# A decode attention and MLP kernel: output weights in longer runs, a reordered last stage, a weights-stationary second MLP layer

## The chip, the cores and the metric

One core of a Trainium2 chip. The time is the device time of one execution in microseconds (us). The kernel before is timed beside every experiment on the same chip, because chips and repeats differ by up to 2.5 us in 690.

"Span" is the stretch from the first to the last instruction in the trace. It is about 2 us shorter than the time.

## The reference, cut to what matters

One token for each of 8 sequences passes through an adaptive layer norm, an attention over a cache of 8192 keys, a projection, a second layer norm and a two-layer MLP.

```python
B, Sq, D = (8, 1, 512); Hq, Hkv, Sk, Dh = (32, 8, 8192, 128); F = 1792
sa, ca, ga, sb, cb, gb = split(_silu(c) @ w_mod)
h = _layernorm(x) * (1 + ca) + sa
q = (h @ wq)                                    # 32 heads, 4 share one key/value head
p = _softmax(q @ k_cache.T * Dh ** -0.5)        # k_cache, v_cache: 8 x 8 x 8192 x 128 bf16 each
x = x + ga * ((p @ v_cache) @ wo)               # wo: 4096 x 512
h = _layernorm(x) * (1 + cb) + sb
x = x + gb * (relu(h @ w1 + b1) ** 2 @ w2 + b2) # w1: 512 x 1792, w2: 1792 x 512
```

The two caches are 268 MB; everything else is about 15 MB.

## The kernel before

The caches are read in 64 units of 4 MB (two heads each; for every sequence four K units, then four V units) through a ring of four slots in SBUF. All large loads are issued by SyncE in one order. wo is loaded once, near the start, in rows of 1 KB:

```python
d_wo = dma("sync", s_wo, lambda e: e.dma_start(wo_sb[:], A_wo.rearrange("(h dh) n -> dh h n", dh=DH)))
```

An ordinary V unit takes 32 matmuls of 512 columns, an eviction to SBUF and four selecting matmuls. The very last V unit is loaded in four pieces (64, 32, 16 and 16 tiles) and done otherwise: 70 matmuls on an identity that do no work ("fillers", put there to keep TensorE's clock up), 128 value matmuls of 8 columns, and between them the part of the output projection that does not need the last unit:

```python
oT_ps = Obank[:, 0:8]
pe_fill(70)
t0 = 0
for i, t1 in enumerate(CH):                      # CH = (64, 96, 112, 128)
    for m in range(t0, t1):
        t = op("tensor", ... matmul(oT_ps, vt[:, m, :], lhs[:, p, 8 * m:8 * m + 8], ...), [loaded[n][i], ...])
    t0 = t1
    if i == 0:
        before_last()                            # 96 projection matmuls, bias matmuls
    elif i == 1:
        pe_fill(8)
# ... normalise, 32 late projection matmuls, layer norm, fillers, first MLP layer: cut ...
for f in range(FT):                              # second layer: the 8 tokens (padded to 64) stationary
    for cc in range(2):
        t = op("tensor", ... matmul(y_ps[64 * cc:64 * (cc + 1), :], hidT[:, f, :],
               W2v[:, f // 2, f % 2, 256 * cc:256 * (cc + 1)], ...), ...)
t = op("vector", ... tensor_tensor(y2, y_ps, gbN[:], ALU.mult), ...)      # gate
t = op("vector", ... tensor_tensor(out_sb, y2, x1N[:], ALU.add), ...)     # residual
# out: one half by SyncE's queue, one by ScalarE's
```

## Time and profile before

| | |
|---|---|
| time, median of 3 (range) | 690.26 us (690.22 to 691.19) |
| span of the profiled run | 689.1 us |
| HBM read | 283.66 MB, 412 GB/s over the span |
| last V unit but one, all of it landed | 656.2 us |
| from there to the end | 32.9 us |
| wo, 4 MB: from the landing of the unit ahead of it to its own | 42.0 to 54.4 us |
| W1, W2 landed / needed | 670.5, 675.0 / 681.4, 683.0 us |

The runs of this kernel fall into two groups, near 690 and near 691 us; the profiled run (690.87) is of the slower group, so its span is about 1 us above the typical one.

Two lines of the page, the span in 40 equal slices of 17.2 us: the busy tenths of the DMA engines and what they moved. Every slice but the first and the last two is full; the third, in which wo is loaded, moves less although it is as busy.

```profile
DMA  8999999999999999999999999999999999999970
GB/s 349 442 365 434 429 431 432 427 432 428 425 434 432 432 426 427 429 426 434 435 430 427 430 425 431 433 428 434 425 435 424 428 432 431 433 430 424 421 312 28
```

The timeline of the end, TensorE's main groups and the store. Columns: start, length of the group in us, engine, line of the program, operation, output and inputs, shape, count, and in brackets the idle time of that engine just before and what ended it.

```profile
656.27 3.60 PE L442 MATMUL PS<-ring,Pm 128*32 128x512 bf16 x32 [3.08 <-DMA ring<-in_A_v_cache_dram]
...
661.46 5.37 PE L340 MATMUL PS<-IDENT 128*128 128x128 bf16 x70
...
666.67 1.75 PE L506 MATMUL PS<-Pm,ring 128*128 128x8 bf16 x64
...
668.28 2.33 PE L478 MATMUL PS<-oTn,wo_sb 128*128 128x8 bf16 x87
672.62 0.38 PE L478 MATMUL PS<-oTn,wo_sb 128*128 128x8 bf16 x9 [2.01 <-issue]
...
676.75 1.02 PE L478 MATMUL PS<-oTn,wo_sb 128*128 128x8 bf16 x32 [0.29 <-DVE oTn L514]
...
681.41 1.68 PE L558 MATMUL PS<-hbT,ring 128*128 128x8 bf16 x56
...
683.02 3.20 PE L566 MATMUL PS<-ring,hidT 128*64 128x256 bf16 x28
...
687.18 0.33 SPq L573 DMA_DIRECT2D out_dram<-P_sb  x1
```

After the last wait for a V unit (first line) TensorE is never kept waiting long by another engine or a transfer: the rest is a serial tail (work in which each step waits for the one before). The fillers run from 661.46 to 666.8, although the first piece of the last V unit has landed at 661.1. Then comes a gap of 2.01 us marked "issue", in which TensorE waits for nothing that the profile shows, in the middle of a row of equal matmuls.

The trace also has a completion mark from each DMA engine for every transfer (read from the trace itself; no view prints them). They are not equal: half of the engines are done 11 us ahead of the other half, and the lag grows over the whole run, from 2 us at 83 us. It grows steadily: over the 58 units in between, the first mark comes every 9.71 us and the last every 9.87. (Marks of the last V unit but one, in us, sorted.)

```
644.6 644.7 644.7 644.7 645.2 645.3 646.2 648.9 | 654.1 655.6 655.6 655.7 655.7 655.8 656.0 656.2
```

Two more lines, of the timeline of SyncE's queue (the issue of w_mod) and of the list of transfers (wo: size, median time from issue to landing):

```profile
1.58 0.37 SPq L191 DMA_DIRECT2D ring<-in_w_mod_dram  x1
...
wo_sb<-in_A_wo_dram SPq DMA_DIRECT2D x1, 4096.0 KB, 50.8
```

### The profile page before, as it was taken

The numbers are of one execution on the slowest core, as the hardware profiler recorded it, in microseconds if no ns is written. First come the engines' busy times: TensorE is split into PE (matmuls) and PEld (weight loads), VectorE is DVE, ScalarE is ACT, GpSimd is POOL, SyncE is SP. The second block draws the span as 40 slices with busy tenths as digits, with TensorE's granted clock in tenths as the row PEclk, the third lists the DMA queues.
The fourth block names the chain that finished last, engine by engine and source line by source line (L and its number), as shares of the span: only waits on it lengthen the run. The fifth ranks groups of instructions, "written<-read, shape, count | busy, mean of one in ns | idle before, by whom it ended". The sixth has DMA issues, their size and how long they took to land.

```text
span 689.1 us, 16075 instructions
## 1 busy us (share of the span) xinstructions
PE 501.7 (73%) x7476; PEld 358.5 (52%) x7476; DVE 300.8 (44%) x557; ACT 235.1 (34%) x281; POOL 17.8 (3%) x67
## 2 busy tenths in 40 slices
PE   2393963897659965798639964698549975699577
PEld 2382731775237731676328741576317752477366
DVE  3161731567116741467216651367215671267302
ACT  1061620465006630366005640265204650156300
POOL 7200000000000000000000000000000000000000
PEclk9997976799659987899659996799857997699865
DMA  8999999999999999999999999999999999999970
GB/s 349 442 365 434 429 431 432 427 432 428 425 434 432 432 426 427 429 426 434 435 430 427 430 425 431 433 428 434 425 435 424 428 432 431 433 430 424 421 312 28
DMA packets 16022, 284.69 MB, mean 413 GB/s; under 512 B 1202, under 2 KB 5331, under 8 KB 6996
## 3 DMA queue, kind: packets, MB, share of 16 engines
q1 hardware_dynamic: 15940, 283.67, 96.7%
q8 instruction: 58, 0.95, 0.6%
q14 instruction: 8, 0.07, 0.0%
q10 hardware_dynamic: 16, 0.00, 0.0%
HBM read 283.66 MB, written 0.01 MB: 412 GB/s over the span
## 4 chain that ended last, share of the span: by engine, by line
PE 54%; DMA 39%; DVE 3%; ACT 2%; issue 1%; SPq 0%
PE PS L348 35%; DMA ring<-in_A_k_cache_dram 34%; PE PS L363 9%; DMA ring<-in_A_v_cache_dram 4%; PE PS L442 4%; PE PS L405 3%; PE PS L340 1%; ACT KTb L353 1%; ACT P_sb L396 1%; DVE Pm L418 1%; DVE m L368 1%; PE PS L423 1%; PE PS L478 1%; PE PS L506 0%; PE PS L566 0%
## 5 line engine op out<-in xcount | busy, mean ns | idle before, releaser
L353 ACT ACTIVATE KTb<-PS 128x1024 bf16<-128x1024 bf16 x192 | 196.5, 1024 | 384.2 <-PE PS L348 384.2
L348 PE MATMUL PS<-IDENT,ring 128*128 128x128 bf16 x4096 | 267.5, 227 | 49.2 <-DMA ring<-in_A_k_cache_dram 49.2
L348 PEld LDWEIGHTS PS<-IDENT,ring 128*128 128x128 bf16 x4096 | 246.9, 102 | 97.7 <-DMA ring<-in_A_k_cache_dram 52.3
L355 DVE COPY KTb<-PS 128x1024 bf16<-128x1024 bf16 x320 | 210.1, 688 | 149.5 <-PE PS L348 147.2
L442 PE MATMUL PS<-ring,Pm 128*32 128x512 bf16 x992 | 88.3, 519 | 51.7 <-DMA ring<-in_A_v_cache_dram 47.4
L363 PE MATMUL PS<-KTb,QTm 128*32 128x512 bf16 x1024 | 78.8, 384 | 4.5 <-ACT KTb L353 4.5
L451 DVE CAST O_sb<-PS 128x512 bf16<-128x512 f32 x31 | 21.4, 692 | 132.5 <-PE PS L442 132.5
L442 PEld LDWEIGHTS PS<-ring,Pm 128*32 128x32 bf16 x992 | 30.8, 121 | 90.2 <-DMA ring<-in_A_v_cache_dram 48.5
L454 PE MATMUL PS<-SEL,O_sb 128*128 128x8 bf16 x124 | 22.6, 182 | 30.4 <-DVE O_sb L451 24.8
L454 PEld LDWEIGHTS PS<-SEL,O_sb 128*128 128x128 bf16 x124 | 12.2, 98 | 59.5 <-DVE O_sb L451 46.1
L405 PE MATMUL PS<-IDENT,P_sb 128*64 128x128 bf16 x512 | 25.7, 276 | 10.3 <-ACT P_sb L396 10.0
L405 PEld LDWEIGHTS PS<-IDENT,P_sb 128*64 128x64 bf16 x512 | 22.1, 147 | 12.9 <-ACT P_sb L396 12.8
L396 ACT ACTIVATE P_sb<-PS,negm 128x512 bf16<-128x512 f32 x32 | 21.5, 685 | 18.9 <-DVE negm L393 18.9
L418 DVE COPY Pm<-PS 64x512 bf16<-64x512 bf16 x48 | 20.1, 421 | 16.6 <-PE PS L405 15.6
L363 PEld LDWEIGHTS PS<-KTb,QTm 128*32 128x32 bf16 x1024 | 15.4, 94 | 21.0 <-ACT KTb L353 8.5
L368 DVE TENSOR_REDUCE m<-PS 128x1 f32<-128x512 f32 x32 | 22.1, 689 | 6.6 <-PE PS L363 6.6
L457 DVE TENSOR_TENSOR oTn<-PS,rinv 128x8 bf16<-128x8 f32 x31 | 6.0, 194 | 31.1 <-PE PS L454 31.1
L542 ACT ACTIVATE std<-PS,epst 128x8 f32<-128x8 f32 x1 | 0.3, 267 | 33.8 <-PE PS L540 33.8
L415 ACT ACTIVATE Pm<-PS 64x512 bf16<-64x512 bf16 x16 | 9.4, 592 | 6.1 <-PE PS L405 5.8
L423 PE MATMUL PS<-rhs_r,ONES 128*128 128x32 f32 x16 | 4.2, 349 | 7.0 <-DVE rhs_r L421 7.0
L309 PE MATMUL PS<-haT,ring 128*128 128x8 bf16 x128 | 3.6, 168 | 7.4 <-DMA ring<-in_A_wq_dram 7.4
L391 PE MATMUL PS<-Dm,R 128*128 128x4 bf16 x8 | 1.4, 179 | 10.1 <-DVE Dm L389 10.1
(103 smaller groups left out, 115.1 us busy)
## 6 DMA issues: line engine op xcount, KB each, us to landing
ring<-in_A_k_cache_dram SPq DMA_DIRECT2D x32, 4096.0 KB, 34.3
ring<-in_A_v_cache_dram SPq DMA_DIRECT2D x31, 4096.0 KB, 29.2
ring<-in_A_wq_dram SPq DMA_DIRECT2D x1, 4096.0 KB, 20.6
wo_sb<-in_A_wo_dram SPq DMA_DIRECT2D x1, 4096.0 KB, 50.8
ring<-in_w_mod_dram SPq DMA_DIRECT2D x1, 3072.0 KB, 10.0
ring<-in_A_v_cache_dram SPq DMA_DIRECT2D x1, 2048.0 KB, 24.6
ring<-in_B_w_dram SPq DMA_DIRECT2D x1, 1792.0 KB, 22.5
ring<-in_A_v_cache_dram SPq DMA_DIRECT2D x1, 1024.0 KB, 26.7
```

What stands on the lines that cost most here:

```text
L348: t = op("tensor", lambda e, j=j, i=i: e.matmul(STG[j][:, i, :], src[:, 32 * k + 8 * j + i, :], IDENT[:, :], is_transpose=True), [loaded[n ...
L353: stg_free[j] = op("scalar", lambda e, j=j, dst=dst: e.activation(dst, STG[j], ACT.Copy), [t])
L355: stg_free[j] = op("vector", lambda e, j=j, dst=dst: e.tensor_copy(dst, STG[j]), [t])
L363: t = op("tensor", lambda e, hf=hf, q=q, rhs=rhs: e.matmul(PS[32 * q:32 * (q + 1), k, :], QTm[:, b, 2 * p + hf, :], rhs, start=(p == 0 and ...
L368: return op("vector", lambda e: e.tensor_reduce(m4[:, k:k + 1], bank(k), AX.X, ALU.max), [t])
L396: exps.append(op("scalar", lambda e, k=k: e.activation(P_sb[:, k, :], bank(k), ACT.Exp, bias=negm[:, 0:1], scale=inv_sqrt, accum_out=rs4[: ...
L405: t = op("tensor", lambda e, k=k, i=i, hf=hf, src=src: e.matmul(STG[k][64 * hf:64 * (hf + 1), i, :], src, IDENT[:, :], is_transpose=True, ...
L418: done.append(op("vector", lambda e, dst=dst, frm=frm: e.tensor_copy(dst, frm), [t, k_pm]))
L423: t = op("tensor", lambda e: e.matmul(tot_ps, ONES[:, :], rhs_r[:]), [t])
L442: t = op("tensor", lambda e, p=p, m=m, cg=cg, vt=vt, Obank=Obank: e.matmul(Obank[32 * cg:32 * (cg + 1), :], lhs[:, p, 32 * m:32 * m + 32], ...
L451: t = op("vector", lambda e, osb=osb, Obank=Obank: e.tensor_copy(osb, Obank), [t])
L454: t = op("tensor", lambda e, i=i, osb=osb, oT_ps=oT_ps: e.matmul(oT_ps, osb[:, i * 128:(i + 1) * 128], SEL[:, i, :], start=(i == 0), stop= ...
```

## The change

Its intent: waste less transfer time on wo, have less work between the last landing and the end, and make the second MLP layer cheaper. c and x are issued by ScalarE, so that SyncE starts with the large loads. Rows of wo are dealt out so that 24 of 32 heads come in runs of 4 KB; 16 small matmuls with a permutation (PERM) then bring the attention output into the same order. The early projection comes ahead of the last V unit, the fillers there go, and three quarters of that unit take the wide form of the other units. The second layer holds the weights stationary and streams 8 columns; its result is transposed at the end. The output went by two queues before as well; now each half has its own copy and leaves as soon as it is copied. The layer norm of the last stage keeps its fillers (20 instead of 16).

```diff
-        d_c = dma("sync", s_c, ...); d_x = dma("sync", s_x, ...)
+        d_c = dma("scalar", s_c, ...); d_x = dma("scalar", s_x, ...)
-        d_wo = dma("sync", s_wo, ... (wo_sb[:], A_wo.rearrange("(h dh) n -> dh h n", dh=DH)))
+        wo_e = wo_sb[:, 0:24, :].rearrange("p (g j) n -> p g (j n)", j=4)
+        d_woe = dma("sync", s_woe, ... (wo_e, A_wo[0:24 * DH, :].rearrange("(g p j) n -> p g (j n)", g=6, p=128)))
+        d_wo = dma("sync", s_wo, ... (wo_sb[:, 24:32, :], A_wo[24 * DH:, :].rearrange("(h dh) n -> dh h n", dh=DH)))
@@ last V unit (cut) @@
-                    pe_fill(70)
-                    # 128 matmuls of 8 columns; 96 early projections after the first 64; pe_fill(8)
+                    # 16 matmuls with PERM, copy to oP, 18 bias matmuls, 96 early projections from oP
+                    for m in range(24):          # 96 of 128 tiles, 512 columns each matmul
+                        t = op("tensor", ... matmul(bank(3)[32 * cg:32 * (cg + 1), :], lhs[...], vt[:, 4 * m:4 * m + 4, :], ...))
+                    t = op("vector", ... tensor_copy(osb, bank(3)), [t])
+                    direct(96, 112, 2, True, False)
+                    # 4 selecting matmuls on osb
+                    t = direct(112, 128, 3, False, True)
@@ second layer and output (cut) @@
-            for cc in range(2): matmul(y_ps[64 * cc:...], hidT[:, f, :], W2v[..., 256 * cc:256 * (cc + 1)], ...)
+            for k in range(KT): matmul(yT_ps[:, k, :], W2v[..., k * 128:(k + 1) * 128], hidT[:, f, :], ...)
+        # gate and residual on 128 x 32, four transposes, two copies (VectorE, ScalarE), two stores
```

## The prediction

> **What bounds it now.** The DMA page strip is at 9 tenths from the second slice to 659 us, 425 to 435 GB/s, 284 MB: the kernel streams the caches at the transfer limit. By the landing marks in the trace, half of the 16 DMA engines land 11 to 12 us after the other half at the end (last-but-one V unit: 644.6 against 656.2 us); the slow half sets the pace. After that landing there is a serial tail of 32.9 us (656.2 to 689.1, the timeline). Its parts: V matmuls 3.6, eviction and selection to 661.8; 70 filler matmuls 661.5 to 666.8, although the last V unit's first piece landed at 661.1; 160 small matmuls; a gap of 2.0 us marked "issue" at 670.6, which coincides with a 16 KB instruction fetch at 670.1 to 671.2; last values and late projection to 677.8; normalisation to 680.9; first MLP layer 681.4 to 683.1; second layer (28 matmuls of 256 columns) to 686.2; two vector operations to 687.15; store and end 1.9. W1 and W2 land at 670.5 and 675.0, needed at 681.4 and 683.0: not critical. The granted clock is 0.50 from 653 to 664 and after 673 (windows).
>
> **The change, step by step.**
> 1. Start: c and x leave SyncE's queue; the w_mod issue moves from 1.58 to about 0.8 us. DMA-bound, so 0.75 us earlier throughout. The Trainium skill (DMA: Bandwidth & Descriptors, "Issuing engines are not separate DMA queues") says that several issuers save only issue time; that is all I count.
> 2. wo: now 12.4 us for 4 MB in 1 KB packets (slow engines, 42.0 to 54.4) against 9.8 for a K unit. Packets of 4 KB take 161 ns against 152 per 4 KB in the 32 KB packets. 3 MB so: 8.1 + 3.1 = 11.2 us. Gain 1.2 to 1.6.
>    Both shift the last-but-one V landing to about 654.05.
> 3. Tail from that landing T (at the half clock, 31 ns a small matmul): V and eviction as before to T+5.6; 16 permutation matmuls 1.0, vector copy 0.4, 96 projections 3.0: T+10.4; 24 V matmuls of 512 columns 2.6: T+13.1; eviction, selection, last 16 value matmuls, normalise: T+15.1; late projection T+16.35; normalisation and fillers about 3.4, first layer 1.7: T+21.4; second layer 56 x 31 ns = 1.75 instead of 3.2: T+23.2; two 32-column vector operations, transposes, copies 1.5 instead of 0.9; store 1.9: T+26.6. Removed on the path: the 70 fillers (5.3 us), most of the instruction-fetch gap. No V piece or weight becomes the wait: they land 2 us earlier too, and W1 keeps about 5 us, W2 about 3.
>
> Span 680.65 instead of 689.1: 8.4 us less. Nearly all of it is on the path: 2.2 from transfers, 6.3 from the tail.
>
> **Predicted: 681.8 us, 679.0 to 685.0 (8 in 10).** Faster by over 2% (under 676.5): 0.03; within 2%: 0.96; slower: 0.01.
>
> **What would show it.** w_mod issue near 0.8 us; wo in two transfers of together about 11 us; last-but-one V landing near 654; no "issue" gap over 1 us in the tail; L569 (second layer) near 1.8 us; landing to end near 26.6 us.
>
> **What would make it wrong.** Instruction fetches stalling TensorE again (the Trainium skill, Runtime: NRT & Kernel Launch, "Instruction fetch mechanics", gives 16 KB blocks of 256 instructions; the trace's 58 packets of 16 KB agree): 1 to 2 us more. A clock at full speed in the tail: 1.5 to 2 us less. W2 landing late if the transfers do not shift. The time saved on wo being absorbed if the fast engines rather than the slow ones profit.

## The result and the profile after

The changed kernel takes 680.42 us (median of 4, 680.02 to 680.49) against 690.24 (689.53 to 691.19) beside it. The ratio is 0.9856, interval 0.9839 to 0.9873. Ratios here are the mean time of one kernel's fast runs over that of the other's of the same rounds, so not quite the ratio of the medians. That is 9.8 us less, 1.4%, within 2% as forecast.

| | before | predicted | after |
|---|---|---|---|
| last V unit but one landed | 656.2 | 654.05 | 653.7 |
| from there to the end of the span | 32.9 | 26.6 | 24.2 |
| wo: landing of the unit ahead to its own | 12.4 | 11.2 | 10.6 |
| span | 689.1 | 680.65 | 677.9 |

The spans differ by 11.2 us, more than the times, because the profiled run of before was one of its slower ones. The sizes in time below come from medians, not from these two spans.

The same two lines of the page after (slices of 16.9 us). The third slice moves 400 GB/s instead of 365, and the end is filled better: the slice before the last has 393 instead of 312.

```profile
DMA  8999999999999999999999999999999999999994
GB/s 365 439 400 434 430 431 433 430 431 425 424 433 429 428 431 433 432 430 431 432 433 425 418 432 430 429 427 431 431 433 432 430 424 426 431 429 431 427 393 160
```

The timeline of the end, after:

```profile
653.78 3.15 PE L438 MATMUL PS<-ring,Pm 128*32 128x512 bf16 x32 [0.88 <-DMA ring<-in_A_v_cache_dram]
...
658.91 0.32 PE L476 MATMUL PS<-oTn,PERM 128*32 128x48 bf16 x16 [0.28 <-DVE oTn L453]
...
659.73 2.64 PE L492 MATMUL PS<-oP,wo_sb 128*128 128x8 bf16 x96
...
662.30 2.75 PE L508 MATMUL PS<-ring,Pm 128*32 128x512 bf16 x24
...
666.84 1.02 PE L525 MATMUL PS<-oTn,wo_sb 128*128 128x8 bf16 x32 [0.29 <-DVE oTn L520]
...
671.27 1.68 PE L561 MATMUL PS<-hbT,ring 128*128 128x8 bf16 x56
...
672.81 0.99 PE L569 MATMUL PS<-hidT,ring 128*128 128x8 bf16 x32
...
674.00 0.81 PE L569 MATMUL PS<-hidT,ring 128*128 128x8 bf16 x24 [0.19 <-DMA ring<-in_B_w_dram]
...
676.08 0.32 SPq L588 DMA_DIRECT2D out_dram<-out_sb  x1
```

The late projection starts at 666.84 instead of 676.75, and no gap marked "issue" stands in TensorE's way any more. The second layer takes 2.0 us instead of 3.2, with a wait of 0.19 us for the last piece of W2, which lands at 674.0.

The queue at the start and wo:

```profile
0.81 0.39 SPq L192 DMA_DIRECT2D ring<-in_w_mod_dram  x1
...
wo_sb<-in_A_wo_dram SPq DMA_DIRECT2D x1, 3072.0 KB, 45.5
wo_sb<-in_A_wo_dram SPq DMA_DIRECT2D x1, 1024.0 KB, 48.0
```

### The profile page after: what moved, and what is told of

It is laid out like the page before. It is cut to its first block, busy times and chain, and to the rows that moved or that the text cites. A ratio compares the mean times of both kernels' runs of the same rounds, so it can differ in the third digit from the quotient of the medians.

```text
span 677.9 us, 15869 instructions
## 1 busy us (share of the span) xinstructions
PE 496.7 (73%) x7372; PEld 352.5 (52%) x7372; DVE 298.4 (44%) x558; ACT 234.9 (35%) x280; POOL 16.7 (2%) x66
## 4 chain that ended last, share of the span: by engine, by line
PE 49%; DMA 45%; DVE 3%; ACT 2%; issue 1%; SPq 0%
DMA ring<-in_A_k_cache_dram 37%; PE PS L344 33%; PE PS L359 8%; DMA ring<-in_A_v_cache_dram 4%; DMA ring<-in_B_w_dram 4%; PE PS L438 3%; PE PS L401 3%; ACT KTb L349 1%; ACT P_sb L392 1%; DVE m L364 1%; PE PS L419 1%; DVE Pm L414 0%; DVE rinv L420 0%; DVE rhs_r L417 0%; DVE Dm L385 0%
## 5 line engine op out<-in xcount | busy, mean ns | idle before, releaser
L349 ACT ACTIVATE KTb<-PS 128x1024 bf16<-128x1024 bf16 x192 | 196.5, 1024 | 378.3 <-PE PS L344 378.3
L359 PEld LDWEIGHTS PS<-KTb,QTm 128*32 128x32 bf16 x1024 | 15.5, 94 | 21.1 <-ACT KTb L349 8.5
```

The source lines that it names most:

```text
L349: stg_free[j] = op("scalar", lambda e, j=j, dst=dst: e.activation(dst, STG[j], ACT.Copy), [t])
L359: t = op("tensor", lambda e, hf=hf, q=q, rhs=rhs: e.matmul(PS[32 * q:32 * (q + 1), k, :], QTm[:, b, 2 * p + hf, :], rhs, start=(p == 0 and ...
```

## The experiments

Twelve runs on the chip. e3 and e7 start from the kernel before, all others from the changed kernel. They ask three things: what each part is worth (e1, e2, e3, e7), what the "issue" gap is (e3, e7, e8), and whether the late half of the DMA engines sets the pace, and can be relieved (e4 to e6, e9, e11).

### e1: wo in 1 KB runs again

```diff
-        d_woe = dma("sync", s_woe, ... (wo_e, A_wo[0:24 * DH, :].rearrange("(g p j) n -> p g (j n)", ...)))
+        for j in range(4):     # same places in SBUF, rows of 1 KB
+            d_woe = dma("sync", s_woe, ... (wo_j[:, :, j, :], wo_r[:, :, j, :]))
```

> The changed kernel with the first 24 heads of wo in 1 KB runs again (four transfers, one for each row of a 4 KB run, same place in SBUF). Theory (short packets cost transfer time, and the slow half of the DMA engines is never short of work): wo takes 12.4 us instead of 10.6, the landing of the last-but-one V unit moves from 653.7 to about 655.4, the time is about 1.7 us longer than the changed kernel, ratio to before about 0.988. Rival (the ring of four slots absorbs it): landing and time as in the changed kernel, ratio 0.9856.

Measured: 681.73 us (681.21 to 681.89), ratio 0.9872. The changed kernel's eight runs (not taken beside this one; four of them surely on another chip) are all between 680.02 and 680.53. wo took 11.9 us (41.4 to 53.3) instead of 10.6, and the last V unit but one landed at 655.1 instead of 653.7. So the landing moved by 1.4 us and the time by 1.3. Nothing was absorbed by the ring: transfer time saved 600 us before the end is still there at the end.

### e2: c and x on SyncE's queue again

```diff
-        d_c = dma("scalar", ...); d_x = dma("scalar", ...)
+        d_c = dma("sync", ...); d_x = dma("sync", ...)
```

> The changed kernel with c and x issued by SyncE again. Theory: w_mod is issued near 1.58 us instead of 0.81, all landings 0.7 us later, time 0.7 us longer, ratio about 0.9866. Rival: the start does not matter, because x then lands earlier (7.9 us in the changed kernel, 2.7 before) and gives the time back: within 0.2 us.

Measured: 680.75 us (680.60 to 680.95), ratio 0.9859. In its timeline the issue of w_mod is back where it was:

```profile
1.56 0.37 SPq L192 DMA_DIRECT2D ring<-in_w_mod_dram  x1
```

The last V unit but one landed at 654.4, 0.7 us later; the time is 0.3 us longer. The landing followed the theory and the time about half of it. The difference is too near the spread of repeats to say where the rest went. x did land late in the changed kernel (7.9 us instead of 2.7), but nothing waited for it that mattered.

### e3: the kernel before without its 70 fillers

```diff
-                    pe_fill(70)
```

> The kernel before without its 70 filler matmuls ahead of the last V unit. Theory (they lie on the path, and the 2.0 us gap is an instruction fetch tied to a place in the instruction stream): the first value matmul starts near 661.8 instead of 666.7; at the half clock the following 160 matmuls take about 0.9 us longer; the gap is not after 87 projection matmuls any more but 221 matmuls after the last selection, or gone; time 4 to 6 us shorter, ratio about 0.993. Rival (the fillers pay for themselves by the full clock they bring, the gap belongs to the projection): time within 1 us of before, the gap again after the 87th projection matmul.

Measured: 684.41 us (684.15 to 684.56) against 690.19, ratio 0.9912. That is 5.8 us, more than half of what the whole change brings, from deleting one line. Its timeline:

```profile
661.20 1.85 PE L505 MATMUL PS<-Pm,ring 128*128 128x8 bf16 x64
...
662.91 2.70 PE L478 MATMUL PS<-oTn,wo_sb 128*128 128x8 bf16 x96
...
668.03 0.32 PE L505 MATMUL PS<-Pm,ring 128*128 128x8 bf16 x5
...
669.11 0.86 PE L505 MATMUL PS<-Pm,ring 128*128 128x8 bf16 x27 [0.75 <-issue]
```

Two things are seen here. First, the value matmuls start at 661.2 instead of 666.67. Second, the gap has left the projection, now whole with 96 matmuls, and stands in the value matmuls. Counted from the last selecting matmuls, it comes after 64 + 96 + 14 + 2 + 32 + 8 + 5 = 221 matmuls. In the kernel before it came after 70 + 64 + 87 = 221. It is tied to a place in the instruction stream, not to an operation.

What the fillers bought is a higher granted clock for the matmuls after them. The windows view, one stretch of each kernel, columns: stretch, length, busy time of the five engines, granted clock, DMA share, GB/s. First before, then e3:

```profile
664.00:668.00 4.00, 4.00 (x101) 4.00 (x100) 0.00 (x0) 0.00 (x0) 0.00 (x0) 0.97 0.76 301
```

```profile
664.00:668.00 4.00, 4.00 (x117) 3.75 (x114) 0.00 (x0) 0.00 (x0) 0.00 (x0) 0.50 0.75 294
```

The Trainium skill (TensorE: Matmul & The Clock Gate, "Why this matters for your kernels") advises to keep TensorE busy for 4 us to get the full clock. With the fillers it comes: 0.50 in 660 to 664, then 0.97. But e3 shows that being busy is not enough: TensorE works without a break from 660.4 to 668.4, 8 us, mostly in matmuls of 8 columns, and the clock stays at 0.50 until 676. Nor is it worth much here: a projection matmul of 8 columns takes 2.33/87 = 26.8 ns at the full clock and 2.70/96 = 28.1 ns at half. For 160 of them that is 0.2 us, bought with 5.4. (The expectation had 0.9 us for this.)

### e4: half of wo on eight DMA engines

```diff
+        for s in range(16):
+            dma("sync", s_woe, ... (wo_e[8 * s:8 * s + 8, 0:4, :], wo_r[8 * s:8 * s + 8, 0:4, :]))
```

> The changed kernel with 2 MB of wo moved by sixteen transfers of 8 partitions each, which run on 8 of the 16 DMA engines alone (the Trainium skill, DMA: Bandwidth & Descriptors, says the lowest-numbered ones). The late half of the engines lands 11 us after the early half at the end of the changed kernel. Theory (the late half sets the pace, by its own rate): if these 8 are the early half, the landing of the last-but-one V unit comes about 5 us earlier (the halves near 648 both) and the time is 675 to 676; if they are the late half, it comes about 5 us later, 685 to 686. Rival (the lag is not the engines' own, but comes from how the ring is filled or how work is shared out): the landing moves by less than 1.5 us either way.

Measured: 695.26 us (694.58 to 701.78), ratio 1.009, slower. The experiment failed as a test. wo was there at 73.6 instead of 51.9 us, because the sixteen transfers themselves were slow and held up everything behind them in SyncE's queue; one stretch of the windows view, while they ran:

```profile
46.00:50.00 4.00, 3.64 (x58) 2.51 (x58) 2.59 (x5) 2.20 (x3) 0.00 (x0) 1.00 1.03 142
```

Busy engines (1.03) moved 142 GB/s. In the profiled run, its slowest, all engines were later at the end, by 16 to 23 us (sorted marks of the last V unit but one, against the changed kernel). This tells nothing about the halves.

### e5 and e6: the same bytes by GpSimd's queue

```diff
+            dma("gpsimd", s_g, ... (DUM[:, s, :], c[:, 0:32]))                          # tiny; e6: after the large one
+            dma("gpsimd", s_g, ... (wo_e[a0:a0 + 29:4, 0:4, :], wo_r[a0:a0 + 29:4, 0:4, :]))
```

> The changed kernel with 2 MB of wo taken off SyncE's queue and issued by GpSimd after its setup, in sixteen transfers of 8 partitions, 4 apart, each behind a tiny transfer of 8 rows of 64 B. By the Trainium skill (DMA: Bandwidth & Descriptors, how many engines) a GpSimd transfer of 8 shares takes 8 consecutive engines from a cursor that moves on, so the tiny ones should take one half of the engines and the large ones always the other. Theory (the late half sets the pace, by its own slower rate, and is the lowest-numbered half, as the last experiment hints): the late half sheds 4.9 us of work and the early half gains as much; the two halves land within 2 us of each other near the end; last-but-one V unit near 649 instead of 653.7; time 675 to 677. If the large ones fall on the late half: V unit near 658.5, time near 685. Rival (the lag comes from the ring or from sharing, not from the engines): spread stays 10 to 12 us and the time within 1 us of 680.4.

> The same with the order turned: the large transfer first, the tiny one after it, so that the large ones fall on the other half of the engines than in e5. Theory: the opposite of e5: if e5 brings the V unit to 649, this brings it to about 658.5, the spread of the halves grows from 11 to about 20 us, time near 685. Rival: the same time as e5.

Measured: 686.61 us (ratio 0.9945) and 686.75 us (0.9949). Both are 6 us slower than the changed kernel and equal to each other; the last V unit but one landed at 660.4 and 660.2, with the spread of the engines still 11 us. The letter of the rival holds (the order does not matter), but not its time. Why the pair did not separate the halves is not shown. By the probe e9 the late engines are not a numbered half (two of them lie in 0 to 7, six in 8 to 15), which makes the test weaker than planned, but does not make the two orders equal; and the trace, whose marks have no engine numbers, can't show that the large transfers fell on the halves as intended.

### e7: the second layer alone, in the kernel before

The edit is the second-layer and output part of the change (with b2 and the gate in transposed form), all else as before.

> The kernel before with the weights-stationary second layer and its output path alone (bias, gate and residual in transposed form, output by transposes and two copies); fillers, projection order, wo and start as before. Theory: second layer 56 small matmuls near 1.8 us instead of 28 of 3.2 us, end of matmuls to store issue 1.3 to 1.5 us instead of 0.9: 0.9 us shorter, ratio 0.9987; the instruction-fetch gap of 2 us moves from after the 87th early projection matmul to after the 95th, because 8 matmuls of the start are gone. Rival (small matmuls save nothing at the half clock, the issue rate binds): no gain, or up to 1 us longer.

Measured: ratio 0.9984, interval 0.9971 to 0.9998; 689.84 us against 690.06. The mean of its six runs is 1.1 us below (one of them at 687.54), the median 0.2. Its timeline:

```profile
668.75 2.53 PE L462 MATMUL PS<-oTn,wo_sb 128*128 128x8 bf16 x95
673.40 0.17 PE L462 MATMUL PS<-oTn,wo_sb 128*128 128x8 bf16 x1 [2.13 <-issue]
...
683.26 1.63 PE L541 MATMUL PS<-hidT,ring 128*128 128x8 bf16 x56
```

The layer takes 1.63 us instead of 3.20, and from its start to the store issue 2.9 us (683.26 to 686.17) instead of 4.2 (683.02 to 687.18). So 1.2 us are saved on the path; the time shows between 0.2 and 1.1, at the limit of what can be told. The gap did as forecast: 8 matmuls fewer at the start put it 8 later, after the 95th projection, at 70 + 64 + 95 = 229.

### e8: the last V unit in small matmuls, in the changed kernel

```diff
-                    for m in range(24): ... matmul(bank(3)[...], lhs[...], vt[:, 4 * m:4 * m + 4, :], ...)
-                    (copy, direct(96, 112), 4 selecting matmuls)
+                    direct(0, 64, 0, True, False)
+                    direct(64, 96, 1, False, False)
+                    direct(96, 112, 2, False, False)
                     t = direct(112, 128, 3, False, True)
```

> The changed kernel with the last V unit done as in the kernel before, 128 value matmuls of 8 columns, instead of 24 of 512 columns plus eviction, selection and 32 of 8 columns; early projection still ahead of it. It keeps 72 more matmuls in a dense stretch. Theory (the wide form pays by keeping TensorE inside the instructions it has already fetched): a gap marked issue of 1 to 2 us falls in the value matmuls, after the 99th of them (229 matmuls after the last selection), and the time is 0.7 to 2 us longer than the changed kernel. Rival (the form does not matter, or the small form is better because it needs no eviction): no such gap, last values ready 0.3 us earlier, time 0 to 0.5 us shorter.

```profile
662.25 2.78 PE L501 MATMUL PS<-Pm,ring 128*128 128x8 bf16 x99
667.39 0.91 PE L501 MATMUL PS<-Pm,ring 128*128 128x8 bf16 x29 [2.35 <-issue]
```

The gap came exactly where the count said, after the 99th value matmul, and was 2.35 us. The time was 681.38 us (680.81 to 681.61; the changed kernel: 680.02 to 680.53), about 1 us longer. By ratio, 0.9859, the two can't be told apart, because the kernel before ran slower beside e8 (691.3). The trace is plainer: from the landing of the last V unit but one to the end 25.3 us instead of 24.2, with a gap of 2.35 in it. Without the gap the small form would be the shorter one, by about 0.5 us (an estimate: from the first value matmul to the late projection 6.34 us less 2.35, against 4.54): it needs no eviction and no selection.

What the gap is: the trace has the transfers that bring instructions, one of 16 KB at a time, 57 to 59 in a whole run, and one of them runs in or just before each gap. In all four TensorE goes on 1.3 to 1.4 us after that transfer has ended.

```
                       gap on TensorE        16 KB instruction transfer
before                 670.61 to 672.62      670.11 to 671.21
e3, no fillers         668.36 to 669.11      666.58 to 667.68
e7, layer 2 alone      671.28 to 673.40      670.95 to 672.06
e8, small values       665.03 to 667.39      664.96 to 666.06
changed kernel         none                  664.37 to 665.48
```

16 KB are 256 instructions of 64 B, by the Trainium skill (Runtime: NRT & Kernel Launch, "Instruction fetch mechanics"), and a matmul with its weight load is two, so a block is 128 matmuls. 221 and 229 are one such block boundary seen from kernels that differ by 8 matmuls at the start: counted from the start of the program, exactly 14,529 of TensorE's records (weight loads, matmuls and the few waits among them) precede the end of the gap in all four kernels. The page says that crossing a boundary is mostly hidden. That holds for most of this kernel. Why not here follows from the record one block (256 records) ahead. In the four kernels the transfer began 2.9 to 3.5 us after that record, and TensorE went on 5.4 to 5.9 us after it. Without the gap it would have been through the block in 3.4 (before and e7), 3.6 (e8) and 4.7 us (e3), and the gap is what was missing: 2.0, 2.1, 2.35 and 0.75 us. In the changed kernel the block holds the 24 wide matmuls and takes 7.2 us; its boundary falls into the filler matmuls of the layer norm, and the next block is there in time.

### e9: which DMA engines are late

```diff
+                    d_prb = [dma("sync", sem(f"d_prb{q}"), ... (PRB[0:q, q - 1, :], A_wq[0:q, 0:32])) for q in range(1, 16)]
```

> The changed kernel with fifteen tiny transfers (1 to 15 rows of 64 B) on SyncE's queue behind the last V pieces[...]. Theory (the late half is one numbered half, the lowest as e4 hinted): transfers of 1 to 8 rows land with late marks alone (about 664 and later), those of 9 to 15 rows have one to seven early marks (about 653). Rival A (the highest half is late): 1 to 8 rows have early marks alone. Rival B (late and early engines alternate in number): early and late marks share each transfer evenly, which would also say why e5 and e6 moved nothing. The time is a few us longer; it is no verdict.

The Trainium skill (DMA: Bandwidth & Descriptors, "Why a DMA increments its semaphore by 16 and not by 1") says that a transfer of k rows from this queue uses the k lowest-numbered engines. The trace agrees in the number, k marks for k rows; which engines they are is the page's word. With that rule, each transfer shows one engine more than the last. Marks of some of them, us:

```
k = 1: 653.4
k = 2: 653.6 654.8
k = 4: 653.9 654.0 655.2 656.8
k = 5: 653.8 654.1 654.1 655.4 657.0
k = 7: 654.2 654.5 654.5 655.7 657.4 663.9 664.1
k = 8: 653.1 654.4 654.7 654.7 655.9 657.6 664.1 664.3
k = 9: 653.3 653.3 654.6 654.8 654.9 656.1 657.8 664.3 664.5
```

Every expectation is missed: neither numbered half is late, nor every other engine, and the one run was no longer than the changed kernel (680.31 us). By this reading engines 0 to 4, 7, 8 and 15 are early, 5, 6 and 9 to 14 are late (9 to 14 each add a mark between 662.2 and 664.4 in the same way; 15 is early because the large transfers have eight early marks and k = 15 has seven). This is one run on one chip; e4 and e11 ran on others.

### e10: the changed kernel again

> The changed kernel itself, unaltered, as the measure for the two runs beside it on the same chip. Expected: ratio to before 0.9856, time 680 to 681 us, last-but-one V unit near 653.7, spread of the engines 11 us there.

Measured: 680.35 us (680.17 to 680.53), ratio 0.9862; landing of the last V unit but one at 653.8, spread 11.2 us. As expected. This run has no wait for W2: its second layer is one group of 56 matmuls in 1.64 us. The wait of 0.19 us in the profile above comes and goes.

### e11: part of wo on the four lowest engines, from ScalarE's queue

```diff
+        for s in range(24):    # 4 partitions, 8 apart
+            d_k4 = dma("scalar", s_k4, ... (wo_e[a0:a0 + 25:8, 0:2, :], wo_r[a0:a0 + 25:8, 0:2, :]))
```

> The changed kernel with 0.75 MB of wo moved to the four lowest-numbered DMA engines, all of them early by the probe e9 (landings of 653.4, 654.8, 653.8 and 656.8 where the late eight had 662 to 664): 24 transfers of 4 partitions, 8 apart, on ScalarE's queue while that engine is idle, so that SyncE's queue is not held up. Theory (the late eight engines set the pace by their own rate, so taking work off them is worth its time on them): each late engine sheds 48 KB, 1.9 us; the four gain 5.9 us and stay no later than the late ones; last-but-one V unit near 651.8, time 1.5 to 2 us shorter than e10. Rival (the lag comes from sharing and moves with the load, or small transfers cost more than they shed, as in e4 to e6): V unit where it is in e10 or later, no gain.

Measured: 687.61 us (686.78 to 687.73), ratio 0.9964: 7 us slower than e10. The last V unit but one landed at 661.0. The load went where it was meant to (by the rule cited under e9, engines 0 to 3): of its eight early marks four now come at 654.1 to 658.8, the other four at 649.9 to 650.5. But the engines that should have been relieved were later, not earlier, by 6 us at 87 us of the run and by 7 at the end. Between 42 and 58 us the engines moved 227 to 298 GB/s at a busy share of 0.69 to 1.01. As in e4 to e6, these transfers beside the stream cost all engines more than they shed. Two causes are not separated: they are small, and they load only a few engines, for which the ring of slots then waits (SyncE could issue the fourth K unit only at 55.9 us, in e10 at 45.1). Whether the late engines' own rate sets the pace therefore stays open as a test: no experiment managed to move work from one group to the other without slowing both. The marks speak for it: after the disturbance the last one again came every 9.87 us and the first every 9.71.

### e12: e11 with W2 in runs of 8 and 6 KB

```diff
-                    w2_r = B_w2.rearrange("(k p j) n -> p k j n", p=128, j=2)
+                    w2_r = B_w2.rearrange("(p j) n -> p j n", p=128)      # hidden unit 14 p + j
-                wcol = ... "p (q j) -> p j q", j=2)[:, f % 2, :]
+                wcol = ... W1v[:, k, :].rearrange("p (q j) -> p j q", j=FT)[:, f, :]
```

> e11 with W2 in runs of 8 and 6 KB instead of 2 KB (hidden units dealt out 14 to a partition, W1 columns and b1 read with step 14 to match). Theory: in the changed kernel the last W2 piece lands at 674.0 just where the second layer needs it (a wait of 0.2 us), so shorter W2 transfers (91 us of 2 KB packets an engine's share against about 82 for long ones, 0.4 us) take that wait away and little more: 0.2 to 0.5 us shorter than e11. Rival: the step of 14 slows the weight loads of the first layer (56 in 1.7 us now) and the time is the same or longer.

(The 91 and 82 us in this text are slips for ns, the time of 2 KB in short and in longer packets.) Measured: 689.81 us (689.47 to 690.11), ratio 0.9997, 2.2 us slower than e11. The first layer of e11, then that of e12:

```profile
679.11 1.68 PE L567 MATMUL PS<-hbT,ring 128*128 128x8 bf16 x56
```

```profile
679.82 3.50 PE L566 MATMUL PS<-hbT,ring 128*128 128x8 bf16 x56
```

The rival was right. Weights read with a step of 14 elements instead of 2 double the layer, from 30 to 62 ns a matmul. And since the last V unit is so late in e11, W2 had slack there that the edit could not use.

No version beat the changed kernel.

## Why the prediction was right

It said 681.8 us, 679.0 to 685.0, within 2%; measured 680.42. The time came out closer than the sum behind it, and that is luck: the span was forecast 2.75 us too long (680.65 against 677.9), but the two profiled runs happened to lie on either side of their medians. Point by point:

- **Bound by transfers until the last V units, then a serial tail.** Right. e1 and e2 moved the landing of the last V unit but one by 1.4 and 0.7 us from edits in the first 55 us. What no experiment shows is the detail that the slow half of the engines sets this by its own rate (e4 to e6 and e11 failed as tests).
- **Start, 0.75 us.** The issue moved to 0.81 and the landing by 0.7 (e2). The time gave 0.3 to 0.4. The skill's rule that several issuers save issue time alone agrees: the two issues that left SyncE's queue took 0.40 and 0.27 us.
- **wo, 1.2 to 1.6 us.** 1.3 to 1.4 (e1).
- **Fillers, 5.3 us.** 5.8 measured (e3), in which the shrinking of the gap from 2.0 to 0.75 us is contained.
- **The gap is instruction fetch.** Right, and shown: in e3, e7 and e8 it stayed at the same record of the program, whatever matmul stood there, with a 16 KB transfer that ended 1.3 to 1.4 us before the gap did. The prediction said "most of" it would go; all of it went.
- **Second layer, 3.2 to 1.75 us, with 0.6 given back for the output.** 1.6 to 2.0; start to store issue 3.3 instead of 4.2 in the changed kernel.
- **Tail 26.6 us.** It was 24.2; this is the term that was mis-sized. "V and eviction as before to T+5.6" measured T+5.2: the V matmuls took 3.15 us instead of 3.6, with the clock still full at their start (to 654.3 in the trace). "16 permutation matmuls 1.0 ... 96 projections 3.0: T+10.4" measured T+8.6: the permutation took 0.32 and the projection 2.64. From there on the sum is right: T+10.4 to T+26.6 was forecast as 16.2 and took 15.5. I had guessed the permutation matmuls at 60 ns; they took 20. I had also taken the half clock, and the windows show 0.79 in 656 to 660 and 0.64 in 660 to 664; but that was worth little, because e8, at 0.50 there, took 0.39 and 2.72 for the same two groups.
- **"W2 about 3" us of slack.** Wrong, without cost. W2 lands only 1.0 us earlier (674.0), not 2, because one engine brings its last share 1.3 us after the others, and the tail got shorter than forecast. The slack is nil: 0.19 us of wait in one profile, none in another. The next saving in this tail will meet W2.

The pieces measured alone give 5.8 (e3), 1.3 (e1), 0.3 (e2) and 0.2 to 1.1 (e7), together 7.6 to 8.5 of the 9.8 us. The rest, some 1 to 2 us, is left for the new order of the last stage; e8 shows about 1 us of it: the wide form has no room for the fetch gap. I did not measure the rest alone.

## What to carry to other kernels

Look first at what stands on the path without doing work: here 70 fillers that bought a clock that the small matmuls after them hardly use were over half of the gain. A gap marked "issue" in a row of equal small matmuls is worth a count: here it stayed at the same number of instructions when the code around it moved, which gave it away as instruction fetch, and fewer, wider matmuls in the block ahead of it took it away. In this kernel, which streams at the transfer limit, transfer time saved early arrived at the last landings in full or nearly so (e1, e2), but transfers on a few engines put beside the stream early in the run cost far more than their bytes.

## What the Trainium skill lacked or had wrong

- Runtime: NRT & Kernel Launch, "Instruction fetch mechanics" says that a block boundary is mostly hidden. It lacks when it is not: where TensorE would have been through a block of 128 mostly small matmuls in 3.4 to 4.7 us while the cache stream was still running, it stood still for 2.01 us (before), 2.13 (e7), 2.35 (e8) and 0.75 (e3); where the block took 7.2 us (changed kernel), it did not.
- TensorE: Matmul & The Clock Gate, "Why this matters for your kernels" asks for 4 us of dense work to get the full clock. In e3, 8 us without a break, mostly matmuls of 8 columns, did not bring it (0.50 throughout). For matmuls of 8 columns the full clock is worth 1.3 ns each here (28.1 against 26.8); 5.4 us of fillers cost 5.8 us of time with what hung on them (e3).
- The same page, "Weight-path perf modes", allows column steps up to 1,024 elements for fast weight loads and lacks what a step costs: 56 matmuls took 1.68 us with weights at step 2 and 3.50 us at step 14 (e12).
- DMA: Bandwidth & Descriptors, "Latency and other measured facts" has engines 7 and 15 as usually slower, with GpSimd's transfers as its guess at the cause. On SyncE's queue here eight of sixteen engines fall 11 us behind in 650 us, and by the probe e9 (one run, one chip) these are 5, 6 and 9 to 14, while 7 and 15 are early. No page has this.
- The same page has transfers under 64 KB as mostly overhead, but not what transfers on a few engines do to the stream beside them: with 2 MB of wo in sixteen transfers of 8 partitions, wo took 29.6 us instead of 10.6, and from 42 to 54 us the engines moved 141 to 145 GB/s at a busy share of 1.03 to 1.06 (e4); by GpSimd's queue the whole run lost 6 us (e5, e6), and 0.75 MB in transfers of 4 partitions from ScalarE's queue cost 7 us (e11).
